# One more row pair of the spatial product by one level of Strassen, with the buffers and the order around it

## The chip, the cores and the metric

The kernel runs on one core of a Trainium2 chip. The metric is the device time of one launch in microseconds (us), as the median of several runs. The engines are named as in the profile: PE is the matrix engine, PEld its weight loads, DVE the vector engine, ACT the scalar engine, POOL the GpSimd engine, and SP the engine that only issues transfers here.

## The reference

Two branches work on the same `x` (2048 tokens x 512) and are mixed by a sigmoid gate per token. Branch A is a linear attention with 32 heads of 16 columns; branch B a gated MLP whose gate mixes tokens with the 2048 x 2048 matrix `w_sp`.

```python
# A: for each head, phi_q and phi_k are softmax(+p) and softmax(-p) of q @ w_phi, k @ w_phi
kv  = einsum('bhsf,bhsd->bhfd', phi_k, v)
z   = einsum('bhsf->bhf', phi_k)
o   = einsum('bhqf,bhfd->bhqd', phi_q, kv) / (einsum('bhqf,bhf->bhq', phi_q, z)[..., None] + 1e-6)
a   = o.reshape(B, S, D) @ wo
# B: z = gelu(x @ w_in), z1 and z2 are its halves of 688 columns
g2  = einsum('ts,bsf->btf', w_sp, layernorm(z2)) + b_sp[None, :, None]
b   = (z1 * g2) @ w_out
g   = sigmoid((x * gate_w).sum(-1))
out = g * a + (1 - g) * b
```

## The kernel before

Tokens are worked on in 16 tiles of 128. There are three stages, and in each the order of PE and of ACT is written out by hand in the Python code, while the order on DVE, POOL and SP is made by a scheduler from priorities.

**First stage** (`z2_tile`, `z1_tile`, `fold`): both halves of `x @ w_in`, gelu, the layernorm of z2 into `z2all` (fp16), the sums of z2's blocks `T1` to `T4` into `zmix`, and `w_phi` folded into the weights of k and q.

**The spatial product** `w_sp @ z2` goes by pairs of row tiles p and p + 8, p = 0 to 7. `w_load` brings both row tiles of a pair, transposed, into one of three buffers `wsp`. A pair in `PLAIN` takes four steps of `plain` (L523), one for each row tile and half of the columns (344), each of 16 matmuls, and DVE adds the bias and multiplies by z1 in place (L531). A pair in `MIXED` takes seven `product`s (L553) of 8 matmuls each, by the Winograd form of one Strassen level. The pair's block matrix is A11, A12 (row tile p) and A21, A22 (row tile p + 8), each 128 rows by 1024 tokens; z2 is cut the same way into B11 to B22. Ahead of its products such a pair needs:

- `w_size` twice (L342): ACT sums absolute values of a half of the pair, one pass over 128 x 2048 each; `w_level` (L351): one small matmul adds over partitions, and DVE makes the factors `wdown` and `wup` (L352, L355); `w_scale` (L370): ACT scales A21 and A22 in place to fp16.
- `w_sum`: S3 = A11 - A21 and S4 = A12 - S2 (L358, DVE), S1 = A21 + A22 (L375, POOL), S2 = A22 - S3 (L377, DVE). S2 and S3 lie in `wmix`.

Three PSUM banks `mm0` to `mm2` hold the products. Products 6, 7 and 4 add onto one bank, and ACT reads it after each of them (`scaled`), so the next one may not start before that read. Product 1 of a following pair is taken between 6 and 7, and `seed` copies it into the second bank. `plus` (DVE) and `gated` (POOL, L573) finish each quarter into z1, which is then called u.

**kv stage**: a loop over 16 tiles. Each turn makes k of the next tile (`k_tile`), v of this one, adds to the 128-wide kv sums (`kv_acc`, two tiles late), and does one entry of `steps`; every second or third turn it makes a tile of q. The steps of pairs 0 to 4 fall here. Step 16 on fall into the output stage.

**Output stage**: first three turns of product, `attn_tile`, `q_tile`; then for each of 16 tiles in pair order (`token`) `ba_tile` (o @ wo and u @ w_out into one bank), one product and one q tile or what is left (`FILL`), `attn_tile` four tiles ahead, and `u_T`. `attn_tile` multiplies q by kv into the bank pair `kvat`, of which there is one only: DVE must have read it (L609, L610) before the next `attn_tile` may write it; before the first one DVE must have taken the kv sums out of it (`kvz_evac`, L500, L505). SP transposes q (`eqT`, L471), o (`oT`, L619) and u (`uT`, L520) by DMA.

In the kernel before, pairs 0 and 5 are in `PLAIN`. Pair 0's four steps are at turns 0 to 3 of the kv stage, pair 5's at the passage from the kv stage to the output stage (three of them each stand ahead of one of the first three `attn_tile`s).

Of the kernel before, what the change touches and what calls it, by code (L numbers as in the profile page):

```python
# [14 lines left out]
P = 128  # L15
# [16 lines left out]
WP = 704  # L32
NP = NT // 2
HS = NT // 2
NRING = 3
PLAIN = (0, 5)
MIXED = (1, 2, 3, 4, 6, 7)
LEVEL = 2.0 ** -15


# [1 line left out]
def kernel(  # L42
# [130 lines left out]
    for p in range(NRING):  # L173
        w_load(p)
    nc.gpsimd.memset(mhalf[:], -0.5)
    nc.gpsimd.memset(mask4[:], 1.0)
# [160 lines left out]
        return [lambda: take(dst[:, 3], banks[3]), lambda: take(dst[:, 2], banks[2])]  # L337

    def w_size(p, h):
        if h == 0:  # L340
            wmix[p] = ring.tile([P, 2, HS, P], FP16, name="wmix", bufs=2)
        nc.scalar.activation(  # L342
            out=wmix[p].bitcast(BF16).rearrange("p k s c -> p (k s c)"),
            in_=wraw[p][:, h * NT:(h + 1) * NT, :].rearrange("p s c -> p (s c)"),
            func=AF.Abs, accum_out=wsum[:, p, h:h + 1])
        if h == 1:
            nc.vector.tensor_tensor(
                out=wsum16[:, p:p + 1], in0=wsum[:, p, 0:1], in1=wsum[:, p, 1:2], op=ALU.add)

    def w_level(p, ps):  # L350
        nc.tensor.matmul(ps[:, 0:1], lhsT=ones_sq[:, :], rhs=wsum16[:, p:p + 1], start=True, stop=True)  # L351
        nc.vector.tensor_scalar(  # L352
            out=wdown[:, p:p + 1], in0=ps[:, 0:1], scalar1=LEVEL, scalar2=1e-30,
            op0=ALU.mult, op1=ALU.max)
        nc.vector.reciprocal(out=wup[:, p:p + 1], in_=wdown[:, p:p + 1])  # L355

    def w_mul_sub(out, raw, p, minus):
        nc.vector.scalar_tensor_tensor(  # L358
            out=out, in0=raw, scalar=wup[:, p:p + 1], in1=minus, op0=ALU.mult, op1=ALU.subtract)

    def w_part(p, name):
        if name in ("S2", "S3"):
# [7 lines left out]
        nc.scalar.activation(out=tail.bitcast(FP16), in_=tail, func=AF.Copy, scale=wup[:, p:p + 1])  # L370

    def w_sum(p, k):
        a21, a22, s2, s3 = (w_part(p, name) for name in ("A21", "A22", "S2", "S3"))
        if k == 1:
            S1_ENG.tensor_tensor(out=a21, in0=a21, in1=a22, op=ALU.add)  # L375
        elif k == 2:
            nc.vector.tensor_tensor(out=s2, in0=a22, in1=s3, op=ALU.subtract)  # L377
        elif k == 3:
            w_mul_sub(s3, w_part(p, "A11"), p, a21)
        else:  # L380
            w_mul_sub(w_part(p, "S4"), w_part(p, "A12"), p, s2)
# [9 lines left out]
    def z_sum(part, i):  # L391
# [5 lines left out]
    S1_ENG = nc.gpsimd  # L397
# [28 lines left out]
    def bank_tile(tag):  # L426
        return psM.tile([P, CH], FP32, name="mm", tag=tag)
# [88 lines left out]
            nc.sync.dma_start(out=w_out_sb[0:REM, 5, :], in_=B_w_out[5 * P:FH, :])  # L516

    def u_T(n):
        uT = work.tile([P, NFT, P], BF16, name="uT", bufs=NUT)
        nc.sync.dma_start_transpose(out=uT[:, :, :], in_=z1all[:, token(n), :])  # L520
        uTs[n] = uT

# [8 lines left out]
        nc.vector.scalar_tensor_tensor(  # L531
            out=zu, in0=x, scalar=bT[:, t:t + 1], in1=zu, op0=ALU.add, op1=ALU.mult)

    LEAD = {6: 1, 7: 1}
    LOAD_AT = {3: 4, 4: 7, 5: 10, 6: 13, 7: 16}
    PRODUCTS = {1: (0, "A11", "B11"), 6: (1, "S2", "T2"), 5: (2, "S1", "T1"), 2: (0, "A12", "B21"),
                7: (1, "S3", "T3"), 4: (1, "A22", "T4"), 3: (2, "S4", "B22")}
    OPENS, SEEDED = (1, 5), (6, 7, 4)
# [58 lines left out]
    def attn_tile(n):  # L597
        at = psM.tile([P, 8, P], FP32, name="at", tag="kvat", bufs=1)
        for g in range(8):
            nc.tensor.matmul(  # L600
                at[:, g, 0:AW], lhsT=eqTs[n][:, g, :], rhs=kvz[:, g, :], start=True, stop=True)
        rden = work.tile([P, 8, NG], FP32, name="rden", tag="rden")
        o = work.tile([P, D], BF16, name="o")
        o_out(n, o[:].rearrange("p (u h d) -> p u h d", u=8, d=DH), at[:, :, 0:AW], rden, NG)
        o_T(n, o)

    def o_out(n, o, at, rden, nh):
# [61 lines left out]
    def at(n, *todo):  # L669
        work_at.setdefault(n, []).append(todo)  # L670

    for p in range(NP):
        n, after = len(steps), MIXED[MIXED.index(p) + 1:][:1] if p in MIXED else ()
        if p in PLAIN:
            steps += [[(plain, t, j)] for t in (p, p + HS) for j in range(2)]
            continue
        opened = p - 1 in MIXED
        follow = [(product, q, 1) for q in after if q == p + 1]
        first = [(product, p, 1)] * (not opened) + [(product, p, 5), (product, p, 2)]
        middle = [(product, p, 6)] + follow + [(product, p, 7)]  # L680
# [9 lines left out]
    for p in range(NRING, NP):  # L690
        at(LOAD_AT[p], w_load, p)

    for i, n in enumerate((1, 2)):
# [7 lines left out]
    def level(n):  # L701
        for f, p, *_ in work_at.get(n, ()):
            if f is w_scale:
                w_level(p, bank_tile(Q_BANK if n < NT else X_TAGS[2]))

    FILL = [("p", "q")] * 6 + [("p", "qp"), ("p", "p")] + [("p", "")] * 4 + [("", "")] * 3
    Q_AT = (1, 3, 6, 9, 12, 15)
    with tc.manual_schedule(engines={mybir.EngineType.PE, mybir.EngineType.Activation}):
        ks = {0: k_tile(0, Q_BANK)}
        kvacc = psM.tile([P, 8, P], FP32, name="kvacc", tag="kvat", bufs=1)  # L710
        pend = []
        for tt in range(NT):
# [7 lines left out]
            pend.append((tt, ek, v_tile(tt, rk, V_BANK if tt != 1 else X_TAGS[2])))  # L720
            level(tt)
            prepare(tt, w_sum)
            if len(pend) == 3:
                kv_acc(*pend.pop(0))
            for i, part in enumerate(steps.pop(0)):
                part[0](*part[1:])
                if i == 0:
                    prepare(tt, w_scale, *[w_size] * late)
            if tt in Q_AT:
                q_tile(Q_AT.index(tt), bank_tile(Q_BANK))  # L730
        nc.scalar.activation(out=g_el[:, :], in_=glog[:, :], func=AF.Exp)
        nc.vector.tensor_scalar(out=g_1p[:, :], in0=g_el[:, :], scalar1=1.0, scalar2=None, op0=ALU.add)
        nc.vector.reciprocal(out=g_inv[:, :], in_=g_1p[:, :])
# [7 lines left out]
    with tc.manual_schedule(engines={mybir.EngineType.PE, mybir.EngineType.Activation}):  # L741
        wo_t = st2.tile([P, NG, D], BF16, name="wo_t", bufs=1)
        nc.gpsimd.dma_start(out=wo_t[:, :, :], in_=A_wo.rearrange("(g p) n -> p g n", p=P))
        todo, done_steps = [], [0]
        x_tags = list(X_TAGS)

        def products(n):
            for _ in range(n):
                if not todo and steps:
                    todo.extend(steps.pop(0))  # L750
                    n = NT + done_steps[0]
                    done_steps[0] += 1
                    level(n)
                    prepare(n, w_sum)
                    f, *args = todo.pop(0)
                    f(*args)
                    prepare(n, w_load, w_size, w_scale)
                elif todo:
                    f, *args = todo.pop(0)
                    f(*args)  # L760
# [62 lines left out]
```

## Time and profile before

| what | value |
|---|---|
| median of three runs | 201.99 us (201.79 to 203.42) |
| the profiled execution's own time | 202.68 us |
| its span | 200.3 us |
| PE busy | 194.9 us, 97% of the span |
| DVE busy | 139.5 us, 70% |
| ACT busy | 126.7 us, 63% |
| POOL busy | 93.0 us, 46% |
| granted PE clock | 1.0 in all of the span |
| L527, matmuls of the plain pairs | 128 |
| L559, matmuls of the mixed pairs | 144 + 96 + 96 |

The span is what the instructions cover; the execution's own time has 2.4 us more around it. A group's "mean ns of one" on PE includes the tail of a pipelined matmul; how long a row of matmuls holds PE is read from the starts in the timeline.

### The profile page before, as it was taken

How to read it: one execution, taken by the hardware profiler on the slowest of the kernel's cores; microseconds unless marked ns; L12 is line 12 of the kernel's file. 1: busy time of each engine (PE TensorE's matmuls, PEld its weight loads, DVE VectorE, ACT ScalarE, POOL GpSimd, SP SyncE). 2: the span in 40 equal slices, each digit the busy share in tenths (PEclk: the TensorE clock that was granted, in tenths of full speed). 3: DMA queues.
4: the chain of work that ended last, by engine and by line, in shares of the span. 5: the costliest groups of instructions: out<-in, count | busy, mean ns of one | idle time of the engine just before them, and what ended most of it. 6: DMA issues, size and time to landing. Idle time of an engine off the chain costs nothing.

```text
span 200.3 us, 3991 instructions
## 1 busy us (share of the span) xinstructions
PE 194.9 (97%) x1473; PEld 116.8 (58%) x1491; DVE 139.5 (70%) x260; ACT 126.7 (63%) x199; POOL 93.0 (46%) x134
## 2 busy tenths in 40 slices
PE   7999999999999999999999999999999999999994
PEld 3666666665555665565565656655555555556542
DVE  4379877914988977887887974999698666633500
ACT  3466667889849759959957469576844455224222
POOL 6021123000665765986985979266058244421300
PEclk9999999999999999999999999999999999999999
DMA  6899489998053930980990844983948988793261
GB/s 183 142 199 217 75 196 198 159 196 236 1 43 77 224 57 0 186 157 0 197 145 3 168 94 119 184 170 69 155 101 170 164 177 168 149 147 78 80 151 58
DMA packets 89210, 26.50 MB, mean 132 GB/s; under 512 B 84536, under 2 KB 89064, under 8 KB 89192
## 3 DMA queue, kind: packets, MB, share of 16 engines
q1 hardware_dynamic: 86448, 23.32, 61.8%
q10 hardware_dynamic: 2600, 2.42, 4.2%
q0 software_dynamic: 144, 0.52, 1.0%
q8 instruction: 11, 0.18, 0.4%
q14 instruction: 7, 0.06, 0.1%
HBM read 3.45 MB, written 2.10 MB: 28 GB/s over the span
## 4 chain that ended last, share of the span: by engine, by line
PE 89%; DVE 4%; ACT 3%; DMA 2%; issue 1%; SPq 0%; DVEq 0%
PE mm L559 24%; PE zp L208 19%; PE mm L434 12%; PE mm L629 10%; PE mm L624 7%; PE mm L477 6%; PE mm L527 6%; PE at L600 2%; DMA w_z<-in_B_w_in_dram 2%; PE kvacc L494 2%; ACT wmix L342 2%; DVE zs L442 1%; DVE o L610 1%; DVE wmix L358 1%; ACT eq L438 0%
## 5 line engine op out<-in xcount | busy, mean ns | idle before, releaser
L208 PE MATMUL zp<-w_z,xT 128*128 128x344 bf16 (+1 forms) x254 | 38.3, 311 | 0.3 <-DMA w_z<-in_B_w_in_dram 0.3
L208 PEld LDWEIGHTS <-xT 128*128 128x128 bf16 x254 | 24.5, 98 | 12.0
L559 PEld LDWEIGHTS <-wsp 128*128 128x128 f16 (+1 forms) x240 | 22.9, 98 | 12.2 <-issue 0.5
L573 POOL TENSOR_TENSOR z1all<-c,z1all 128x344 bf16<-128x344 f32 x24 | 22.8, 960 | 15.2 <-DVE c L566 11.7
L641 ACT ACTIVATE ob<-mm,g_inv 128x512 bf16<-128x512 f32 (+1 forms) x16 | 10.9, 681 | 22.6 <-PE mm L629 20.0
L559 PE MATMUL mm<-z2all,wsp 128*128 128x344 f16 x144 | 23.9, 309 | 0.0
L442 DVE TENSOR_REDUCE zs<-ek 128x64 f32<-128x1024 bf16 x16 | 19.0, 1193 | 7.0 <-ACT ek L438 7.0
L438 ACT ACTIVATE eq<-mm 128x512 bf16<-128x512 f32 x32 | 17.3, 594 | 10.3 <-PE mm L434 6.5
L442 DVE TENSOR_REDUCE zs<-eq 128x64 f32<-128x1024 bf16 x16 | 19.4, 1214 | 5.7 <-ACT eq L438 5.5
L629 PE MATMUL mm<-w_out_sb,uT 128*128 128x512 bf16 (+2 forms) x101 | 23.3, 366 | 0.1
L342 ACT ACTIVATE wmix<-wsp 128x2048 bf16<-128x2048 bf16 x12 | 23.0, 1918 | 0.0
L527 PE MATMUL mm<-z2all,wsp 128*128 128x344 f16 x128 | 20.0, 309 | 0.0
L375 POOL TENSOR_TENSOR wsp<-wsp 128x1024 f16<-128x1024 f16 x6 | 12.8, 2126 | 13.8 <-DVE wmix L358 13.8
L457 POOL TENSOR_TENSOR ratio<-zs,rk 128x32 f32<-128x32 f32 x16 | 7.5, 466 | 23.7 <-DVE rk L451 21.1
L434 PEld LDWEIGHTS <-xT 128*128 128x128 bf16 x128 | 11.8, 98 | 10.5
L438 ACT ACTIVATE ek<-mm 128x512 bf16<-128x512 f32 x32 | 17.3, 601 | 1.1 <-PE mm L434 1.1
L458 POOL TENSOR_TENSOR eq<-eq,ratio 128x512 bf16<-128x512 bf16 x16 | 16.9, 1058 | 1.3
L458 POOL TENSOR_TENSOR ek<-ek,ratio 128x512 bf16<-128x512 bf16 x16 | 16.9, 1059 | 0.0
L223 ACT ACTIVATE z2raw<-zp 128x688 bf16<-128x688 f32 x16 | 11.8, 744 | 7.6 <-PE zp L208 7.3
L629 PEld LDWEIGHTS <-uT 128*128 128x128 bf16 x102 | 9.8, 98 | 11.2 <-DMA uT<-z1all 0.2
L624 PE MATMUL mm<-wo_t,oT 128*128 128x512 bf16 (+2 forms) x66 | 16.3, 366 | 0.1
L434 PE MATMUL mm<-wk_p,xT 128*128 128x512 bf16 x61 | 16.1, 379 | 0.2
(100 smaller groups left out, 322.8 us busy)
## 6 DMA issues: line engine op xcount, KB each, us to landing
out_dram<-ob ACTq DMA_DIRECT2D x14, 128.0 KB, 2.6
w_z<-in_B_w_in_dram SPq DMA_DIRECT2D x2, 344.0 KB, 5.1
w_out_sb<-in_B_w_out_dram SPq DMA_DIRECT2D x1, 640.0 KB, 5.4
wv_sb<-in_A_wqkv_dram SPq DMA_DIRECT2D x1, 512.0 KB
wo_t<-in_A_wo_dram POOLq DMA_DIRECT2D x1, 512.0 KB, 4.5
w_z<-in_B_w_in_dram ACTq DMA_DIRECT2D x2, 172.0 KB, 3.9
w_z<-in_B_w_in_dram SPq DMA_DIRECT2D x2, 172.0 KB, 4.0
wsp<-in_B_w_sp_dram SPq DMA_TRANSPOSE x16, 5.2
```

Of the source, the lines that this page charges most:

```text
L208: nc.tensor.matmul(zp[:, j, 0:n], lhsT=xT[:, dt, tt * P:(tt + 1) * P], rhs=wt[:, dt, j * HF:j * HF + n], start=(dt == 0), stop=(dt == NDT ...
L342: nc.scalar.activation(out=wmix[p].bitcast(BF16).rearrange("p k s c -> p (k s c)"), in_=wraw[p][:, h * NT:(h + 1) * NT, :].rearrange("p s ...
L375: S1_ENG.tensor_tensor(out=a21, in0=a21, in1=a22, op=ALU.add)
L434: nc.tensor.matmul(ps[:, :], lhsT=xT[:, dt, tt * P:(tt + 1) * P], rhs=w[:, dt, :], start=(dt == 0), stop=(dt == NDT - 1))
L438: nc.scalar.activation(out=e[:, :, a, :], in_=ps[:, :].rearrange("p (h f) -> p h f", f=DH), func=AF.Exp, scale=1.0 - 2.0 * a)
L442: nc.vector.tensor_reduce(out=z[:].rearrange("p h a -> p (h a)"), in_=e[:].rearrange("p h a f -> p (h a) f"), axis=AX.X, op=ALU.add,)
L458: nc.gpsimd.tensor_tensor(out=e[:, :, 1, :], in0=e[:, :, 1, :], in1=ratio[:, :, None].to_broadcast([P, H, DH]), op=ALU.mult)
L527: nc.tensor.matmul(x, lhsT=wraw[t % HS][:, h * NT + st, :], rhs=z2all[:, st, j * HF:(j + 1) * HF], start=(st == 0), stop=(st == NT - 1))
L559: nc.tensor.matmul(x, lhsT=w_part(p, wa)[:, st, :], rhs=zsums[zb][:, st, :], start=(k in OPENS and st == 0), stop=(st == HS - 1), skip_gro ...
L573: nc.gpsimd.tensor_tensor(out=zu, in0=o, in1=zu, op=ALU.mult)
L624: nc.tensor.matmul(acc, lhsT=oTs[n][:, g, :], rhs=wo_t[:, g, c0:c1], start=start and g == 0, stop=stop and g == NG - 1)
L629: nc.tensor.matmul(acc, lhsT=uTs[n][:, ft, :], rhs=w_out_sb[:, ft, c0:c1], start=start and ft == 0, stop=stop and ft == NFT - 1)
```

## The change

Pair 5 moves from `PLAIN` to `MIXED`. All of pairs 1 to 7 now chain: each pair's product 1 stands between products 6 and 7 of the pair before, so pair 5's product 1 is in the kv stage, and the output stage has 20 products (pairs 5, 6 and 7) in place of four plain steps and 14 products. In the passage one product stands ahead of the first `attn_tile` and two ahead of the second and third.

- There are four `wsp` buffers in place of three, and pairs 3 to 7 are loaded three turns earlier. `w_size` writes its unused result into a buffer of its own (`mute`), not into `wmix`, and `wmix` is taken when S3 is formed. The turns of `w_size` and `w_scale` are moved.
- `uT` and `oT` move to the pool `st2`, which takes the room that the kv stage's pools leave. The transfers that fill them can then not start in the kv stage.
- S3 and S4 are formed in two halves each. S1 of pair 6 is formed by DVE, the others still by POOL.
- `wdown` and `wup`, `kvz_evac` and the two DVE operations of `attn_tile` get high priority for the scheduler. The gate's factors are formed at turn 2 of the kv stage.
- `FILL` and the places of the level matmul are adapted.

```diff
-NRING = 3
-PLAIN = (0, 5)
-MIXED = (1, 2, 3, 4, 6, 7)
+NRING = 4
+PLAIN = (0,)
+MIXED = (1, 2, 3, 4, 5, 6, 7)
...
-        if h == 0:
-            wmix[p] = ring.tile([P, 2, HS, P], FP16, name="wmix", bufs=2)
+        mute = ring.tile([P, NT * P], BF16, name="mute", bufs=1)
         nc.scalar.activation(
-            out=wmix[p].bitcast(BF16).rearrange("p k s c -> p (k s c)"),
+            out=mute[:, :],
...
     def w_mul_sub(out, raw, p, minus):
-        nc.vector.scalar_tensor_tensor(
-            out=out, in0=raw, scalar=wup[:, p:p + 1], in1=minus, op0=ALU.mult, op1=ALU.subtract)
+        for c in (slice(0, HS // 2), slice(HS // 2, HS)):
+            nc.vector.scalar_tensor_tensor(
+                out=out[:, c, :], in0=raw[:, c, :], scalar=wup[:, p:p + 1], in1=minus[:, c, :],
+                op0=ALU.mult, op1=ALU.subtract)
...
     def w_sum(p, k):
+        if k == 3:
+            wmix[p] = ring.tile([P, 2, HS, P], FP16, name="wmix", bufs=2)
...
         if k == 1:
-            S1_ENG.tensor_tensor(out=a21, in0=a21, in1=a22, op=ALU.add)
+            (nc.vector if p == 6 else nc.gpsimd).tensor_tensor(out=a21, in0=a21, in1=a22, op=ALU.add)
...
-        uT = work.tile([P, NFT, P], BF16, name="uT", bufs=NUT)
+        uT = st2.tile([P, NFT, P], BF16, name="uT", bufs=NUT)
...
-    LEAD = {6: 1, 7: 1}
-    LOAD_AT = {3: 4, 4: 7, 5: 10, 6: 13, 7: 16}
+    LOAD_AT = {3: 1, 4: 4, 5: 7, 6: 10, 7: 13}
+    SIZE_AT = {1: (0, 1, 2), 2: (2, 3, 4), 6: (14, 16, 17), 7: (18, 19, 20)}
...
-        o_out(n, o[:].rearrange("p (u h d) -> p u h d", u=8, d=DH), at[:, :, 0:AW], rden, NG)
+        with tc.high_priority():
+            o_out(n, o[:].rearrange("p (u h d) -> p u h d", u=8, d=DH), at[:, :, 0:AW], rden, NG)
...
-        oT = work.tile([P, NG, P], BF16, name="oT", bufs=7)
+        oT = st2.tile([P, NG, P], BF16, name="oT", bufs=7)
...
-        n -= LEAD.get(p, 0)
-        at(n - 4, w_size, p, 0)
-        at(n - 3, w_size, p, 1)
-        at(n - 2, w_scale, p)
+        s0, s1, s2 = SIZE_AT.get(p, (n - 5, n - 4, n - 3))
+        at(s0, w_size, p, 0)
+        at(s1, w_size, p, 1)
+        at(s2, w_scale, p)
...
-                w_level(p, bank_tile(Q_BANK if n < NT else X_TAGS[2]))
+                w_level(p, bank_tile(K_BANK if NT <= n < NT + 4 else Q_BANK))
 
-    FILL = [("p", "q")] * 6 + [("p", "qp"), ("p", "p")] + [("p", "")] * 4 + [("", "")] * 3
+    FILL = [("p", "q")] * 7 + [("p", ""), ("p", "p"), ("p", ""), ("p", ""), ("p", "p")] + [("", "")] * 3
...
-        kvz_evac()
+        with tc.high_priority():
+            kvz_evac()
...
         for n in range(3):
-            products(1)
+            products(1 + (n > 0))
             attn_tile(n)
             q_next()
```

More of the change, by code (lines that the diff above doesn't have):

```diff
@@ L171, in w_load @@
                 out=wraw[p][:, h * NT:(h + 1) * NT, :], in_=B_w_sp[t * P:(t + 1) * P, :])
-    for p in range(NRING):
+    for p in range(3):
         w_load(p)
@@ L351, in w_level @@
         nc.tensor.matmul(ps[:, 0:1], lhsT=ones_sq[:, :], rhs=wsum16[:, p:p + 1], start=True, stop=True)
[L352 to L355, printed above, removed]
+        with tc.high_priority():
+            nc.vector.tensor_scalar(
+                out=wdown[:, p:p + 1], in0=ps[:, 0:1], scalar1=LEVEL, scalar2=1e-30,
+                op0=ALU.mult, op1=ALU.max)
+            nc.vector.reciprocal(out=wup[:, p:p + 1], in_=wdown[:, p:p + 1])
     def w_mul_sub(out, raw, p, minus):
-        nc.vector.scalar_tensor_tensor(
-            out=out, in0=raw, scalar=wup[:, p:p + 1], in1=minus, op0=ALU.mult, op1=ALU.subtract)
+        for c in (slice(0, HS // 2), slice(HS // 2, HS)):
+            nc.vector.scalar_tensor_tensor(
+                out=out[:, c, :], in0=raw[:, c, :], scalar=wup[:, p:p + 1], in1=minus[:, c, :],
+                op0=ALU.mult, op1=ALU.subtract)
     def w_part(p, name):
@@ L395, in z_sum @@
             out=zsums[out][:, c, :], in0=zsums[a][:, c, :], in1=zsums[b][:, c, :], op=op)
-    S1_ENG = nc.gpsimd
     with tc.manual_schedule(engines={mybir.EngineType.PE, mybir.EngineType.Activation}):
@@ L685 @@
             at(n + lag, w_sum, p, k)
-        n -= LEAD.get(p, 0)
-        at(n - 4, w_size, p, 0)
-        at(n - 3, w_size, p, 1)
-        at(n - 2, w_scale, p)
-    for p in range(NRING, NP):
+        s0, s1, s2 = SIZE_AT.get(p, (n - 5, n - 4, n - 3))
+        at(s0, w_size, p, 0)
+        at(s1, w_size, p, 1)
+        at(s2, w_scale, p)
+    for p in range(3, NP):
         at(LOAD_AT[p], w_load, p)
@@ L720 @@
             pend.append((tt, ek, v_tile(tt, rk, V_BANK if tt != 1 else X_TAGS[2])))
+            if tt == 2:
+                nc.scalar.activation(out=g_el[:, :], in_=glog[:, :], func=AF.Exp)
+                nc.vector.tensor_scalar(
+                    out=g_1p[:, :], in0=g_el[:, :], scalar1=1.0, scalar2=None, op0=ALU.add)
+                nc.vector.reciprocal(out=g_inv[:, :], in_=g_1p[:, :])
             level(tt)
@@ L724 @@
                 kv_acc(*pend.pop(0))
-            for i, part in enumerate(steps.pop(0)):
+            parts = steps.pop(0)
+            for i, part in enumerate(parts):
                 part[0](*part[1:])
                 if i == 0:
-                    prepare(tt, w_scale, *[w_size] * late)
+                    prepare(tt, *[w_size] * late)
+                if i == 0:
+                    prepare(tt, w_scale)
             if tt in Q_AT:
                 q_tile(Q_AT.index(tt), bank_tile(Q_BANK))
-        nc.scalar.activation(out=g_el[:, :], in_=glog[:, :], func=AF.Exp)
-        nc.vector.tensor_scalar(out=g_1p[:, :], in0=g_el[:, :], scalar1=1.0, scalar2=None, op0=ALU.add)
-        nc.vector.reciprocal(out=g_inv[:, :], in_=g_1p[:, :])
         for p_ in pend:
             kv_acc(*p_)
-        kvz_evac()
+        with tc.high_priority():
+            kvz_evac()
     kvp_cm.__exit__(None, None, None)
@@ L748, in products @@
             for _ in range(n):
-                if not todo and steps:
+                opening = not todo
+                if not todo:
+                    if not steps:
+                        return
                     todo.extend(steps.pop(0))
-                    n = NT + done_steps[0]
                     done_steps[0] += 1
[L753 to L760, printed above, removed]
+                now = NT + done_steps[0] - 1
+                if opening:
+                    level(now)
+                    prepare(now, w_sum)
+                f, *args = todo.pop(0)
+                f(*args)
+                if opening:
+                    prepare(now, w_size)
+                if not todo:
+                    prepare(now, w_scale)
         def q_next():
```

## The prediction

> **What bounds the kernel now.** I read the busy table first, then the waits of PE, then the windows of the passage from the kv stage to the output stage (busy us of each engine in stretches of 4 us), then the timeline there.
>
> ```profile
> PE 194.9 (97%) x1473; PEld 116.8 (58%) x1491; DVE 139.5 (70%) x260; ACT 126.7 (63%) x199; POOL 93.0 (46%) x134
> ```
>
> ```profile
> PE zp L239 <- PEq L807: 0.8, 1, 0.8
> PE at L600 <- DVE o L610: 0.4, 1, 0.4
> PE zp L208 <- DMA w_z<-in_B_w_in_dram: 0.3, 1, 0.3
> ```
>
> ```profile
> 124.00:128.00 4.00, 3.95 (x34) 2.56 (x33) 3.75 (x10) 1.75 (x6) 2.16 (x4) 1.00 0.96 120
> 128.00:132.00 4.00, 4.00 (x34) 2.57 (x33) 3.84 (x8) 3.56 (x5) 1.47 (x3) 1.00 1.24 255
> 132.00:136.00 4.00, 3.57 (x30) 2.15 (x29) 4.00 (x8) 2.98 (x6) 2.77 (x2) 1.00 0.58 115
> 136.00:140.00 4.00, 4.00 (x32) 2.31 (x30) 3.90 (x10) 2.27 (x4) 2.49 (x4) 1.00 0.37 71
> ```
>
> In the windows the columns are PE, PEld, DVE, ACT and POOL. PE is the bound. Between the first loads and the end it waits once, in the passage, and there DVE is busy for 15.5 of 16 us. So time can be had only by fewer matmuls or by that one wait, and DVE in the passage has no room. The wait in the timeline:
>
> ```profile
> 130.68 2.50 PE L527 MATMUL mm<-z2all,wsp 128*128 128x344 f16 x16
> 130.77 1.97 DVE L358 SCALAR_TENSOR_TENSOR wmix<-wsp,wup 128x1024 f16<-128x1024 bf16 x1
> ...
> 132.67 0.74 DVE L610 SCALAR_TENSOR_TENSOR o<-at,g_el,rden 128x512 bf16<-128x512 f32 x1
> ...
> 133.56 0.42 PE L600 MATMUL at<-kvz,eqT 128*128 128x68 bf16 x8 [0.38 <-DVE o L610]
> ...
> 137.00 0.42 PE L600 MATMUL at<-kvz,eqT 128*128 128x68 bf16 x8
> ```
>
> The third `attn_tile` (at2, counting from 0) could have started at 130.68 + 2.33 = 133.01; it started at 133.56, 0.15 us after DVE's o ended at 133.41. **0.55 us** were lost. The reader should see why: S3 (L358) took 1.97 us where the other five took 1.28, and o stood behind it. The fourth (at3) started at 137.00. From at3 on both kernels have the same PE work: 14 products, the same attention, q and output tiles. PE has no wait there before. So **the change is worth what at3 moves**, plus any new wait later.
>
> **PE's work.** Row starts give what a group holds PE: 8 matmuls of 344 columns 1.17 us (112.28 to 113.44), 16 of them 2.33, k, v or q 0.86, `kv_acc` or `attn_tile` 0.26, the level matmul 0.03. Pair 5 goes from 64 matmuls to 56: 8 x 0.146 = **-1.17**, with one more level **+0.03**. If the old wait of 0.55 went as well and none came, the change would be worth -1.69.
>
> **Until the kv stage ends.** Before, turn 13 has products 5, 2 and 6 and k of tile 15 starts at 115.78. After, product 6 stands in turn 14, so that k starts at 114.61, and PE goes on with v (115.47), kv (116.33), pair 4's product 6 (116.59), pair 5's product 1 (117.76), pair 4's product 7 (118.92), v of tile 15 (120.09), kv (120.95). Product 4 could start at 121.2. It waits for ACT to have read product 7, and ACT has between the reads of 6 and 7 a `w_size` (1.90, and 0.20 for its sum): 117.76 + 0.2 to start + 0.64 + 2.1 + 0.64 = 121.35. Turns 8 and 11 have that order too, but there a k tile of 0.86 covers it; turn 15 has no k. **+0.2**. Then products 4 and 3, q, two kv sums: 125.1. Product 5 of pair 5 covers `kvz_evac`: 0.2 to start, 0.68 and 0.18, done at 126.2; at0 at 126.3 (before 126.08).
>
> The rest of pair 5's preparation in the kv stage I cost at nothing. ACT gets two `w_size` and a `w_scale` (6.2 us) in turns 11 to 13; the pattern is that of turns 5 to 10, where the trace of before has the same operations over three turns and no wait of PE. S1 on POOL (2.13) has from about 119.7 to 125.1. The level matmul stands right behind a q tile in turns 4, 7, 10 and 13 and needs that q's bank; before, ACT was done with q at 96.70 in the turn like it and v ended at 96.84, so this cover is thin: 0 to +0.1 each time. I take 0. Each `w_load` goes into the buffer of the pair that ended one turn before it, three turns ahead of where it was, and SP has then no uT in its queue. The gate's factors (0.22 on ACT, 0.4 on DVE) and a `w_size` of pair 2 fall into turn 2, where ACT stood idle 2.98 us until its `w_scale` at 59.32; the buffer `mute` is written by ACT alone. If that idle time were not there, 2.3 us of ACT would stand ahead of turn 3's k, which is used a turn (5 us) later.
>
> **From at0 to at3, DVE's queue.** In the order of the changed program DVE has, from the end of `kvz_evac` to the o that frees the bank for at3: three sums of q (L442, a start-to-start of 1.2 each) 3.6; three reciprocals of them, 0.28 each, 0.85; three rden at 0.33, 1.0; three o at 0.68, 2.1; wdown and wup 0.35; one `plus` 0.45; S4 of pair 5 in two halves 1.25. Sum **9.6**: 126.2 + 9.6 = 135.8, and with the 0.15 from above at3 starts at 135.95. PE alone would be there at 126.3 + 9.23 = 135.5 (three at, three q, five products, a level). The plain tiles' multiply (0.5 each) is gone from DVE, but 1.17 us of PE's work, its cover, went too. at3 moves from 137.00 to 135.95: **-1.05**, if nothing on DVE is stretched.
>
> S4 may be. Its row:
>
> ```profile
> L358 DVE SCALAR_TENSOR_TENSOR wsp<-wsp,wup,wmix x6: 1179/1236/2150, 69.5 to 174.5; 128x1024 f16<-128x1024 bf16 x6
> ```
>
> The 2150 ns one started at 69.48, at the same time as a POOL multiply (69.49, 1.06 us). Three of the eighteen operations of S2, S3 and S4 are stretched so (1.97, 2.15, 1.75). Unstretched is one end, +0.97 (2.15 - 1.18) the other. By the walk POOL's multiply of q runs from about 128.4 to 129.4, and the first half of S4 would start at 128.7; so I take the middle, **+0.5**. S3, S2 and S1 of pair 6 follow at3 and have cover: S1 on DVE (no row shows it; bounds 0.62 of S2 and 2.13 of POOL's S1) ends some 5.6 us after at3 starts, and the product that needs it comes 6.85 after.
>
> The Trainium skill, "SBUF — State Buffer", section "Who interferes with whom", speaks against this change: a DVE instruction with two SBUF inputs and a GpSimd instruction that reads SBUF exclude each other, and the later waits for the whole of the earlier. The rows above agree in kind. By that rule each half of S4 could be held by a multiply of its own, 2.1 us in all, and at3 would come at 138.0, +1.0; by the rows of stretched whole operations it comes at 136.9, -0.1.
>
> **uT and oT.** The first `uT` waits for the kv sum of tile 13 (121.4) and v's multiply. SP then issues five uT (1.24 each, with gaps 1.3), 121.4 to 128; then q's transpose, ready from POOL at 129.4, then the first oT at 130.8, which lands in 2.6 us (median of L619): 133.4. The first `ba_tile` wants it at 136.2. Slack 2.8. At the end `uT` of tile 14 is wanted 5.16 us after the last product, before it was 5.42 (now the last `attn_tile` stands ahead of that product); the trace needs 1.79 to its issue (188.37 to 190.16) and 3.1 to land, so 0.3 is left: 0.
>
> **Sum.** -1.05 + 0.5 = **-0.55** against the profiled execution: 202.68 becomes 202.1, its span 200.3 becomes 199.75. That execution lies 0.7 over the median; on the median 201.99 - 0.55 gives **201.4**. The forecast's own range is 200.9 to 202.0.
>
> **Rivals.**
> - *PE is fed all through.* DVE's order may fit better than my walk, and the waits go. For it: S4 and S3 were unstretched in ten of twelve. Against it: DVE's 9.6 against PE's 9.23. at3 at 135.5: -1.5, **200.5**.
> - *DVE and POOL block each other in the passage.* One mechanism: six more POOL multiplies (0.84 each) and two more DVE operations with both inputs in SBUF, in a queue that is full. S4 stretched costs 0.97 ahead of at3; after it S3's two halves and S1 stretched by up to 1.0 each end S1 at 5.6 + 3.0 = 8.6 after at3, and product 5 of pair 6, wanted at 6.85, is 1.75 late: -1.05 + 0.97 + 1.75 = +1.7. With two of the three stretched +0.7. Middle **203.0**. It decides from the point where S1 of pair 6 ends over 6.85 us after at3. Against it: only three of eighteen such rows.
> - *SP's queue is late.* Four of the uT behind a busy ring take 2.1 us as one did at 156.31, and the first oT stands behind them and behind q's transpose. 5 x 2.2 from 121.4 ends at 132.4, oT issues at 133.8 and lands at 136.4 to 137.2 (3.4 is the longest): up to 1.0 on the forecast, **202.3**. Against it: the last `wsp` load, which filled the rings at 122.6 to 128.9 before, now is over by then.
>
> That the products aren't fewer can be left out: the built program has 392 + 64 such matmuls in place of 336 + 128.
>
> **Chances.** Forecast 0.50, PE fed 0.15, DVE against POOL 0.18, SP 0.09, something that I don't see 0.08. The range **200.3 to 203.0** leaves out the outer half of the third case, most of the last, and a little below. About 1%, 2.0 us, is what a measurement of this kernel can tell from no change. Faster by that needs under 199.97, more than the whole -1.69: 0.03. Slower needs over 204.0, the far end of the third case or the unseen: 0.12. Within: 0.85.
>
> **What the profile would show.** Right: no wait of PE over 0.3 us in the kv stage; at3 near 136.4; PE's only wait in the passage an `attn_tile` on DVE's o; L561 with 392 matmuls. Wrong: a wait of a product on DVE's S1 or S3, of a `ba_tile` on oT or uT, or of the level matmul on ACT.

## The result, and the profile after

The changed kernel takes 203.09 us (median of 22 runs, 202.62 to 204.39) against 201.96 us of the kernel before: a ratio of **1.005** with a 95% interval of 1.0033 to 1.0068. The forecast was 201.4. The kernel got half a per cent slower, although the eight matmuls that were to be saved are saved.

In this document GpSimd is the profile's POOL and VectorE its DVE. First the busy table and the waits of PE after the change (us in total, times, longest).

```profile
PE 193.5 (96%) x1466; PEld 115.6 (57%) x1484; DVE 152.3 (75%) x279; ACT 134.6 (67%) x209; POOL 96.4 (48%) x138
```

```profile
PE mm L561 <- DVE c L568: 1.2, 2, 0.7
PE mm L350 <- DVE wsum L346: 0.9, 1, 0.9
PE zp L239 <- PEq L820: 0.8, 1, 0.8
PE pq L310 <- DMA gaterow<-in_gate_w_dram: 0.7, 1, 0.7
PE zp L208 <- DMA w_z<-in_B_w_in_dram: 0.6, 1, 0.6
```

PE is busy 1.4 us less. The wait of an `attn_tile` on DVE's o, the only one that PE had behind the first loads before, is gone. Two new lines stand on top: products that wait for `plus` (L568), and a level matmul that waits for a size (L346). The other three lie in the first stage. To see where they lie I cut PE's timeline at three places: the start of the first k tile, the first `attn_tile` (at0) and the fourth (at3).

| kernel | median us | ratio to before (95%) | first k to at0 | at0 to at3 | at3 to the end of the last matmul |
|---|---|---|---|---|---|
| before | 201.96 | 1 | 81.86 | 10.92 | 60.45 |
| after | 203.09 | 1.005 (1.0033 to 1.0068) | 84.04 | 9.33 | 60.44 |
| after, second profile (a2) | 203.26 | 1.0048 (1.0011 to 1.0084) | 84.07 | 9.33 | 60.70 |
| e1: size added by a reduce | 201.72 | 0.9973 (0.9949 to 0.9996) | 82.67 | 9.34 | 60.71 |
| e2: size of pair 2 a turn later | 203.91 | 1.0083 (1.0059 to 1.0106) | 84.93 | 9.34 | 60.43 |
| **e3: every S1 on DVE** | **199.72** | **0.9867 (0.9828 to 0.9906)** | 81.56 | 9.34 | 60.44 |
| e4: S3, S4 whole | 201.08 | 0.9959 (0.9922 to 0.9996) | 81.62 | 9.21 | 60.85 |
| b1: before, every S1 on DVE | 201.38 | 0.9962 (0.9947 to 0.9977) | 81.32 | 10.91 | 60.45 |
| b2: before, S3 and S4 in halves | 205.70 | 1.0171 (1.0145 to 1.0198) | 84.00 | 12.19 | 60.43 |
| e8: e3 and an idle add on POOL | 206.08 | 1.0198 (1.0178 to 1.0218) | 87.19 | 9.33 | 60.44 |
| e9: e3 and an idle copy on POOL | 201.02 | 0.9946 (0.9924 to 0.9968) | 82.61 | 9.33 | 60.44 |
| e13: S1 of 1, 2, 5, 6 on DVE | 200.45 | 0.9916 (0.9889 to 0.9944) | 81.54 | 9.33 | 60.45 |
| e10: e3 with pair 5 plain | 204.26 | 1.0124 (1.0077 to 1.0171) | 81.87 | 16.48 | 58.97 |
| e11: e3 and e4 | 200.49 | 0.992 (0.9893 to 0.9947) | 81.62 | 9.21 | 61.18 |

A run named e changes the kernel after, a run named b the kernel before. Each ratio is to runs of the kernel before that were taken beside it on the same chip (their medians: 201.96 for after, 202.09 for e1 to e4, 202.23 for b1, b2, e8 and e9, 202.12 for the other four). The three stretches are read from one profiled execution of each kernel.

So the passage gained 1.59 us, and the kv stage, where PE's work is the same but for one level matmul (0.03) and the preparation of the pairs was rearranged, lost 2.18. Against e3, in which PE has the same order of work, the loss is visible tile by tile (v tiles counted from the first k): 1.18 us in turn 4, 0.45 in turn 6, 0.86 in turn 15, nothing elsewhere. These are 2.49 in all; e3 itself is 0.30 below the kernel before in this stage.

The timeline of the kernel after around turn 4, all engines (start, us, engine, line, operation; in brackets the idle time before):

```profile
64.78 2.12 POOL L379 TENSOR_TENSOR wsp<-wsp 128x1024 f16<-128x1024 f16 x1 [3.07 <-issue]
...
65.04 1.88 DVE L346 TENSOR_TENSOR wsum<-wsum 128x1 bf16<-128x1 f32 x1
65.11 1.03 PE L479 MATMUL mm<-wv_sb,xT 128*128 128x512 bf16 x4
...
67.07 0.16 PE L350 MATMUL mm<-wsum,ones_sq 128*128 128x1 bf16 x1 [0.93 <-DVE wsum L346]
```

The reader should look at the second line. It adds two columns of 128 numbers, one element for each partition, and takes 1.88 us; the shortest of its seven executions takes 98 ns. It starts inside POOL's S1 and ends at 66.92, POOL's S1 at 66.90. In the kernel before, S1 of this pair ran from 62.72 to 64.84 and the size of pair 2 was added at 69.40, in 0.16 us:

```profile
62.72 2.12 POOL L375 TENSOR_TENSOR wsp<-wsp 128x1024 f16<-128x1024 f16 x1 [2.01 <-DVE wmix L358]
...
69.40 0.16 DVE L347 TENSOR_TENSOR wsum<-wsum 128x1 bf16<-128x1 f32 x1 [0.36 <-ACT wmix L342]
```

The same in turn 15 of the kernel after, with S2 (L381) in the place of the size, and `plus` (L568) behind it:

```profile
122.00 2.12 POOL L379 TENSOR_TENSOR wsp<-wsp 128x1024 f16<-128x1024 f16 x1 [0.63 <-DVE wmix L359]
122.31 2.37 DVE L381 TENSOR_TENSOR wmix<-wsp,wmix 128x1024 f16<-128x1024 f16 x1
...
123.19 1.33 PE L561 MATMUL mm<-zmix,wsp 128*128 128x344 f16 x8
...
124.60 0.56 DVE L568 SCALAR_TENSOR_TENSOR c<-mm,wdown,u 128x344 f32<-128x344 f32 x1
125.22 1.04 PE L561 MATMUL mm<-z2all,wsp 128*128 128x344 f16 x6 [0.69 <-DVE c L568]
```

S2 takes 2.37 us, and again it ends (124.68) soon after POOL's S1 (124.12): the 0.56 us between them are a little less than the 0.62 of the shortest free S2. Product 3 could have started 1.17 after product 4, at 124.36, and started at 125.22. The trace's answer for S2 alone, min/median/max in ns, then the first and last start:

```profile
L381 DVE TENSOR_TENSOR wmix<-wsp,wmix x7: 676/1770/2367, 67.3 to 169.3; 128x1024 f16<-128x1024 f16 x7
```

Six of the seven take over 1.5 us; before, the median was 682 ns. The first, at 67.33 (1.51 us), runs beside POOL's multiply of k and not beside S1; the other five run beside S1.

### The profile page after: what moved, and what is told of

Same layout as the page of the kernel before. It is cut to its first block, busy times and chain, and to the rows that moved or that the text cites. A ratio compares the mean times of both kernels' runs of the same rounds, so it can differ in the third digit from the quotient of the medians.

```text
span 201.8 us, 4016 instructions
## 1 busy us (share of the span) xinstructions
PE 193.5 (96%) x1466; PEld 115.6 (57%) x1484; DVE 152.3 (75%) x279; ACT 134.6 (67%) x209; POOL 96.4 (48%) x138
## 4 chain that ended last, share of the span: by engine, by line
PE 79%; DVE 9%; issue 4%; ACT 4%; DMA 2%; DVEq 0%
PE mm L561 23%; PE zp L208 18%; PE mm L436 10%; PE mm L632 10%; PE mm L627 7%; PE mm L479 4%; PE mm L529 2%; DVE zs L444 2%; DMA gaterow<-in_gate_w_dram 2%; PE at L602 2%; DVE vr L485 1%; PE kvacc L496 1%; DVE wmix L359 1%; DVE wmix L381 1%; ACT ek L440 1%
## 5 line engine op out<-in xcount | busy, mean ns | idle before, releaser
L561 PEld LDWEIGHTS <-wsp 128*128 128x128 f16 (+1 forms) x280 | 26.7, 98 | 15.5 <-issue 1.6
L575 POOL TENSOR_TENSOR z1all<-c,z1all 128x344 bf16<-128x344 f32 x28 | 25.2, 905 | 13.6 <-DVE c L568 7.2
L561 PE MATMUL mm<-z2all,wsp 128*128 128x344 f16 x168 | 27.9, 309 | 1.2 <-DVE c L568 1.2
L341 ACT ACTIVATE mute<-wsp 128x2048 bf16<-128x2048 bf16 x14 | 26.8, 1914 | 0.4 <-ACT ob L644 0.4
L459 POOL TENSOR_TENSOR ratio<-zs,rk 128x32 f32<-128x32 f32 x16 | 7.0, 437 | 25.6 <-DVE rk L453 20.3
L561 PE MATMUL mm<-zmix,wsp 128*128 128x344 f16 x112 | 18.6, 309 | 0.0
L561 PE MATMUL mm<-zmix,wmix 128*128 128x344 f16 x112 | 18.6, 309 | 0.0
L372 ACT ACTIVATE wsp<-wsp,wup 128x2048 f16<-128x2048 bf16 x7 | 14.0, 2000 | 5.6 <-DVE wup L355 5.6
L460 POOL TENSOR_TENSOR ek<-ek,ratio 128x512 bf16<-128x512 bf16 x16 | 17.4, 1085 | 0.0
L479 PE MATMUL mm<-wv_sb,xT 128*128 128x512 bf16 x62 | 16.3, 379 | 0.1
```

The source lines that it names most:

```text
L341: nc.scalar.activation(out=mute[:, :], in_=wraw[p][:, h * NT:(h + 1) * NT, :].rearrange("p s c -> p (s c)"), func=AF.Abs, accum_out=wsum[: ...
L460: nc.gpsimd.tensor_tensor(out=e[:, :, 1, :], in0=e[:, :, 1, :], in1=ratio[:, :, None].to_broadcast([P, H, DH]), op=ALU.mult)
L479: nc.tensor.matmul(v_ps[:, :], lhsT=xT[:, dt, tt * P:(tt + 1) * P], rhs=wv_sb[:, dt, :], start=(dt == 0), stop=(dt == NDT - 1))
L561: nc.tensor.matmul(x, lhsT=w_part(p, wa)[:, st, :], rhs=zsums[zb][:, st, :], start=(k in OPENS and st == 0), stop=(st == HS - 1), skip_gro ...
L575: nc.gpsimd.tensor_tensor(out=zu, in0=o, in1=zu, op=ALU.mult)
```

## The theory and its rivals

**T:** while POOL reads SBUF, a DVE operation with two inputs in SBUF does not run. The change moved S1 (POOL) so that it now runs at the same time as the size of pair 2 (turn 4) and as S2 ahead of `plus` (turns 6 and 15), and PE waits soon after for what stands behind them. **R1:** the size is asked for a turn too early, and POOL has nothing to do with it. **R2:** it is the order and the splitting on DVE alone. **R3:** the first stage got longer too (first k at 44.88 us after, 44.22 before). **R4:** S1 on DVE is simply faster, whatever the change. **R5:** S1's cost is by what waits for its result or by its place in POOL's queue, and no operation of DVE gets longer by it.

## Experiments

### e1: the size added with one input

```diff
-            nc.vector.tensor_tensor(
-                out=wsum16[:, p:p + 1], in0=wsum[:, p, 0:1], in1=wsum[:, p, 1:2], op=ALU.add)
+            with nc.allow_low_precision("sum of two"):
+                nc.vector.tensor_reduce(
+                    out=wsum16[:, p:p + 1], in_=wsum[:, p, 0:2], op=ALU.add, axis=mybir.AxisListType.X)
```

> One edit to the changed kernel: the two halves of a w_sp row's size are added by a tensor_reduce over the pair of columns (one input in SBUF) instead of a tensor_tensor (two inputs in SBUF); the order on every engine stays. Theory T (in the kv stage GpSimd's S1 now runs beside VectorE operations with two SBUF inputs that PE soon waits for): the size of pair 2 takes 0.1 to 0.3 us instead of 1.88 although S1 of pair 1 still runs, the level matmul of turn 4 follows the v tile without its wait, everything after it is 1.0 to 1.1 us earlier: ratio to the kernel before 1.000 (0.998 to 1.002). The waits of products 3 in turns 6 and 15 stay. Rival R1 (the size is asked for a turn too early, GpSimd has nothing to do with it): the wait of the level matmul stays near 0.9 us, ratio 1.005.

It took 201.72 us, 1.4 less than the changed kernel; at0 came 1.37 us earlier. The timeline of e1 at the same place:

```profile
63.90 2.13 POOL L380 TENSOR_TENSOR wsp<-wsp 128x1024 f16<-128x1024 f16 x1 [3.07 <-issue]
64.16 0.09 DVE L347 TENSOR_REDUCE wsum<-wsum 128x1 bf16<-128x2 f32 x1
...
64.65 1.92 DVE L382 TENSOR_TENSOR wmix<-wsp,wmix 128x1024 f16<-128x1024 f16 x1
...
65.08 0.17 PE L351 MATMUL mm<-wsum,ones_sq 128*128 128x1 bf16 x1
```

The same sum, at the same point in DVE's order, in the middle of the same S1, takes 0.09 us when its two numbers come in as one operand, and the level matmul waits for nothing. R1 falls. The next operation with two operands, S2, is held in its place (1.92), where PE does not wait for it. The waits for `plus` stay (1.0 us), as expected.

### e2: the size of pair 2 a turn later

```diff
-    SIZE_AT = {1: (0, 1, 2), 2: (2, 3, 4), 6: (14, 16, 17), 7: (18, 19, 20)}
+    SIZE_AT = {1: (0, 1, 2), 2: (3, 4, 5), 6: (14, 16, 17), 7: (18, 19, 20)}
```

> One edit to the changed kernel: SIZE_AT of pair 2 is (3, 4, 5) as in the kernel before, so its level matmul stands in turn 5. T and R1 both expect the wait of turn 4 to go: ratio to the kernel before 0.999 to 1.001 (1.0 to 1.1 us less than the changed kernel), provided the size is not met by S1 of pair 1 again (S1 is at 64.8 to 66.9 us from the span's start, the size a turn later, near 70). If the wait only moves to turn 5 or to the scaling that stands behind it, ratio 1.003 to 1.005. The waits of products 3 in turns 6 and 15 stay.

A miss: 203.91 us, slower than the changed kernel. The scheduler laid out DVE anew, and the meeting moved to the next pair, in turn 7:

```profile
81.10 2.12 POOL L379 TENSOR_TENSOR wsp<-wsp 128x1024 f16<-128x1024 f16 x1 [1.22 <-ACT mute L341]
81.35 1.89 DVE L346 TENSOR_TENSOR wsum<-wsum 128x1 bf16<-128x1 f32 x1
...
83.39 0.16 PE L350 MATMUL mm<-wsum,ones_sq 128*128 128x1 bf16 x1 [0.34 <-DVE wsum L346]
```

Two products also wait for ACT (0.9 us together): in turn 5 a size of pair 3 and the scaling of pair 2 now stand one behind the other, 73.51 to 77.39, ahead of the read that product 4 needs. With a scheduler between the code and the engine, moving one operation is not one edit.

### e3: every S1 on DVE

```diff
-            (nc.vector if p == 6 else nc.gpsimd).tensor_tensor(out=a21, in0=a21, in1=a22, op=ALU.add)
+            nc.vector.tensor_tensor(out=a21, in0=a21, in1=a22, op=ALU.add)
```

> One edit to the changed kernel: S1 of every pair on VectorE (1.12 us there for the one that is already there) instead of GpSimd (2.12 us for each of five in the kv stage); VectorE gets some 6 us more work in the kv stage and the order of the rest stays nearly as it is. T: the size of pair 2 takes 0.1 to 0.2 us, S2 0.7 us, the halves of S3 and S4 near 0.7; the wait of the level matmul in turn 4 goes (-1.1 us) and those of products 3 in turns 6 and 15 shrink by the difference of 2.37 and 0.7 + 1.1 (-0.4 to -0.6 each): ratio to the kernel before 0.995 to 0.998. Rival R2 (it is the order on VectorE, S2 ahead of the sum with the decoded bank and S3 in two halves with other work between them; more work there makes it worse): waits stay or grow, ratio 1.005 to 1.015.

199.72 us, ratio 0.9867, below what T expected, and **2.4 us faster than the kernel before**. The list of PE's waits has one line left, in the first stage:

```profile
PE zp L239 <- PEq L820: 0.8, 1, 0.8
```

Turn 15, in e3's timeline:

```profile
119.83 0.62 DVE L379 TENSOR_TENSOR wsp<-wsp 128x1024 f16<-128x1024 f16 x1
120.38 0.75 DVE L381 TENSOR_TENSOR wmix<-wsp,wmix 128x1024 f16<-128x1024 f16 x1
...
121.05 0.56 DVE L568 SCALAR_TENSOR_TENSOR c<-mm,wdown,u 128x344 f32<-128x344 f32 x1
121.87 1.33 PE L561 MATMUL mm<-z2all,wsp 128*128 128x344 f16 x8
```

S1 and S2 together take less on DVE (1.22 us to the start of `plus`) than S2 alone did beside POOL's S1 (2.29). DVE's busy time falls from 152.3 to 148.2 us, although it does six more operations. R2, which expected more work on DVE to make it worse, falls in that form.

### e4: S3 and S4 in one instruction again

```diff
-        for c in (slice(0, HS // 2), slice(HS // 2, HS)):
+        for c in (slice(0, HS),):
```

> One edit to the changed kernel: S3 and S4 are one instruction each again instead of two halves (VectorE's order is planned anew; S1 of pair 1 can then start some 2 us earlier, as in the kernel before, 62.7 instead of 64.8 us). T: what counts is whether S1 runs beside the size of pair 2, so the wait of turn 4 goes or shrinks to 0.2 us (-0.9 to -1.1 us), those of turns 6 and 15 stay, the passage is up to 0.3 us worse: ratio 0.999 to 1.003. R1: wait in turn 4 stays, ratio 1.005 to 1.007.

201.08 us, below what either theory expected: all the waits of the kv stage are gone, those of turns 6 and 15 too, which I had expected to stay. With whole operations the scheduler makes another order; in turn 6 it puts S3 of pair 2 ahead of S4 of pair 1, and S1 starts 2.8 us ahead of S2 in place of 1.0. Timeline of e4 there:

```profile
71.96 1.85 DVE L359 SCALAR_TENSOR_TENSOR wsp<-wsp,wup,wmix 128x1024 f16<-128x1024 bf16 x1
72.69 3.10 POOL L379 TENSOR_TENSOR wsp<-wsp 128x1024 f16<-128x1024 f16 x1
75.46 0.89 DVE L381 TENSOR_TENSOR wmix<-wsp,wmix 128x1024 f16<-128x1024 f16 x1
```

Here the one that comes later is POOL: S1 starts at 72.69, but S4 runs until 73.81, and so S1 takes 3.10 us. It ends at 75.79 and holds S2 for 0.2 us only. In turn 15 S2 starts first (119.09, 0.78 us), and S1 (119.28) is the one held: it takes 2.57. So the split is what brought S1 and S2 together, through the order that came of it, and the hold is the price: R2 is right about the cause of the meeting.

### b1 and b2: one part alone in the kernel before

```diff
-    S1_ENG = nc.gpsimd
+    S1_ENG = nc.vector
```

> The kernel before with one edit: S1 of every pair on VectorE, as in the run e3 of the changed kernel. Theory T (S1 on GpSimd holds VectorE operations that PE waits for, in the changed kernel alone; in the kernel before S2 stands behind the sum with the decoded bank and the size behind S1's end, so PE never waits): no gain to be had here, 201.5 to 202.4 us, ratio 0.998 to 1.002. Rival R4 (S1 on VectorE is worth some 2.4 us by itself, and the seventh pair brings nothing even with the waits gone): ratio 0.985 to 0.992.

201.38 us, ratio 0.9962: more than T's none, far less than R4's 2.4 us. At0 comes 0.54 us earlier, in three steps of 0.18 (turns 6, 9 and 12): the old kernel lost a little to S1 on POOL too, in gaps too small for the list of waits. Between b1 and e3 stands the change without S1's holds: 201.38 to 199.72, with intervals of the ratios that do not touch. In the trace 0.24 us are lost in the kv stage (0.19 of them in turn 6) and 1.57 won in the passage.

```diff
-        nc.vector.scalar_tensor_tensor(
-            out=out, in0=raw, scalar=wup[:, p:p + 1], in1=minus, op0=ALU.mult, op1=ALU.subtract)
+        for c in (slice(0, HS // 2), slice(HS // 2, HS)):
+            nc.vector.scalar_tensor_tensor(
+                out=out[:, c, :], in0=raw[:, c, :], scalar=wup[:, p:p + 1], in1=minus[:, c, :],
+                op0=ALU.mult, op1=ALU.subtract)
```

> The kernel before with one part of the change alone: S3 and S4 in two halves each. S2 still stands behind the sum with the decoded bank on VectorE, and S1 of pair 1 does not move (both halves of that S3 stand together). T: S1 comes up to 0.7 us later in the other pairs, S2 is held for it up to 0.7 us, nothing of it reaches PE: ratio 0.999 to 1.003. Rival R2 (the split by itself is what costs the 2 us that undoing it gave back in e4): ratio 1.006 to 1.012.

205.70 us, ratio 1.0171: both theories were far too low. The list of PE's waits in b2:

```profile
PE at L602 <- DVE o L612: 1.6, 1, 1.6
PE mm L561 <- ACT u L543: 1.5, 2, 0.8
```

S2 is held by S1 here as well (79.08, 1.68 us), but that is not the path. Half of an S4 stands ahead of a k tile's reciprocal now and takes 1.40 us beside a multiply on POOL; the factor wup comes 0.63 us later (89.67 against 89.04), ACT starts the pair's scaling later by as much, and ACT's read of product 7 stands behind the scaling: product 4 waits 0.74. In the passage half of an S3 (1.44) makes o late. So the split in itself costs 3.5 us in the old order; in the changed kernel the factor has high priority, and this path does not show.

### e8 and e9: an operation that nobody waits for

```diff
-            (nc.vector if p == 6 else nc.gpsimd).tensor_tensor(out=a21, in0=a21, in1=a22, op=ALU.add)
+            nc.vector.tensor_tensor(out=a21, in0=a21, in1=a22, op=ALU.add)
+            if p != 6:
+                extra = ring.tile([P, HS, P], FP16, name="extra", bufs=1)
+                nc.gpsimd.tensor_tensor(out=extra[:, :, :], in0=a22, in1=s3, op=ALU.add)
```

> The run e3 (S1 on VectorE, 199.72 us) with one thing added: GpSimd adds A22 and S3 of pairs 1, 2, 3, 4, 5, 7 into a tile that nobody reads, in the place on GpSimd where S1 stood, with the same shapes; VectorE's order is that of e3 to the last instruction. T: VectorE operations with two SBUF inputs are held by it as by S1: size of pair 2 near 1.8 us, S1 and S2 on VectorE together held once, and the waits of the level matmul in turn 4 and of products 3 in turns 6 and 15 come back, the latter longer by S1's own 0.7 us: ratio to the kernel before 1.002 to 1.010 (+3 to +4.7 us over e3). Rival R5 (S1 cost by what waits for its result, or by the place in GpSimd's queue ahead of the products with z1, not by holding VectorE): ratio 0.985 to 0.991, no operation of VectorE longer than in e3.

206.08 us, 6.4 above e3 and more than T's upper end. Turn 4 and turn 9 of e8:

```profile
64.10 2.12 POOL L382 TENSOR_TENSOR extra<-wsp,wmix 128x1024 f16<-128x1024 f16 x1 [3.06 <-issue]
64.35 1.88 DVE L346 TENSOR_TENSOR wsum<-wsum 128x1 bf16<-128x1 f32 x1
...
92.46 2.12 POOL L382 TENSOR_TENSOR extra<-wsp,wmix 128x1024 f16<-128x1024 f16 x1 [0.62 <-DVE wmix L359]
92.77 2.36 DVE L379 TENSOR_TENSOR wsp<-wsp 128x1024 f16<-128x1024 f16 x1
...
96.34 0.89 PE L564 MATMUL mm<-z2all,wsp 128*128 128x344 f16 x5 [0.50 <-DVE c L571]
```

No result of `extra` is used, and the size takes 1.88 us, to the digit as in the changed kernel; S1 (L379) is held in S2's stead in five more places. PE waits for the size (0.9) and four times for `plus` (3.4 together), now in turns 9 and 12 too. R5 falls: DVE's operations are what got longer, and PE waits for them. It is the hold.

```diff
-                nc.gpsimd.tensor_tensor(out=extra[:, :, :], in0=a22, in1=s3, op=ALU.add)
+                nc.gpsimd.tensor_copy(out=extra[:, :, :], in_=s3)
```

> As the run e8, but GpSimd's extra instruction is a copy of S3 into the tile that nobody reads (one input in SBUF) in place of the addition. T as the page on SBUF states it (any GpSimd instruction that reads SBUF holds a VectorE instruction with two SBUF inputs): held as in e8, in proportion to the copy's length, ratio above that of e3 by 0.5 to 2%. If only GpSimd instructions with two inputs do it: 0.986 to 0.990 as e3, with the size at 0.1 us and S2 near 0.7 us beside the copy.

201.02 us, 1.3 above e3. A POOL instruction with one input holds as well, for as long as it runs itself:

```profile
63.91 1.04 POOL L382 COPY extra<-wmix 128x1024 f16<-128x1024 f16 x1 [3.00 <-DVE wmix L359]
64.23 0.73 DVE L346 TENSOR_TENSOR wsum<-wsum 128x1 bf16<-128x1 f32 x1
```

The size ends at 64.96, the copy at 64.95. That is what the Trainium skill, "SBUF — State Buffer", section "Who interferes with whom", states of a GpSimd instruction that reads SBUF, and it agrees with e1's reduce too: by that section a VectorE instruction with one SBUF input does not contend with GpSimd, outside the modes that use two ports, and a `tensor_reduce` has none of these on this chip.

### a2, e13, e10, e11

a2 is the changed kernel unaltered.

> The changed kernel as it is, for a second profile. Its first k tile began at 44.88 us in the first profile and at 43.99 to 44.34 in every other kernel, in a stage whose code is the same. If that is a matter of one execution, the first k tile begins at 44.0 to 44.4 here, the stretch from there to the first attention tile is 84.0 again and the passage 9.3. Rival R3 (the change makes the first stage longer): 44.7 or later again. Ratio 1.003 to 1.007.

The first k began at 44.01 us this time; 84.07 and 9.33 came again. R3 falls.

```diff
-            (nc.vector if p == 6 else nc.gpsimd).tensor_tensor(out=a21, in0=a21, in1=a22, op=ALU.add)
+            (nc.gpsimd if p in (3, 4, 7) else nc.vector).tensor_tensor(out=a21, in0=a21, in1=a22, op=ALU.add)
```

> The changed kernel with S1 on VectorE for pairs 1, 2, 5 and 6 (as it was for 6) and on GpSimd for 3, 4 and 7. T in numbers: e3 gained 1.18 us in turn 4 (pair 1), 0.45 in turn 6 (pair 2) and 0.86 in turn 15 (pair 5) over the changed kernel and nothing in turns 9 and 12 (pairs 3 and 4), although S2 takes 2.37 us there; so 2.49 us are gained here as in e3: first attention tile 81.5 to 81.7 us after the first k tile, ratio 0.986 to 0.991. If what the holds cost adds up over all pairs: a third of the gain is missing, ratio 0.991 to 0.996.

At0 comes 81.54 us after the first k: all of e3's gain in the kv stage, with three pairs still on POOL. The ratio, 0.9916, lies just inside the range of the other expectation, and its interval takes in both; I go by the trace, since the time between its first k and its end is that of e3 to 0.1 us. In turn 9 of e13:

```profile
89.68 2.13 POOL L379 TENSOR_TENSOR wsp<-wsp 128x1024 f16<-128x1024 f16 x1 [0.63 <-DVE wmix L359]
89.98 2.37 DVE L381 TENSOR_TENSOR wmix<-wsp,wmix 128x1024 f16<-128x1024 f16 x1
...
92.28 0.56 DVE L568 SCALAR_TENSOR_TENSOR c<-mm,wdown,u 128x344 f32<-128x344 f32 x1
92.89 1.33 PE L561 MATMUL mm<-z2all,wsp 128*128 128x344 f16 x8
```

S2 is held for its full 2.37 us, and product 3 still follows product 4 (91.72) after 1.17. A hold costs only where its cover is gone.

```diff
-PLAIN = (0,)
-MIXED = (1, 2, 3, 4, 5, 6, 7)
+PLAIN = (0, 5)
+MIXED = (1, 2, 3, 4, 6, 7)
```

> The run e3 with the seventh pair undone: rows 5 and 13 of w_sp by plain products again (64 matmuls of 344 columns instead of 56), the rest of the change as it is, S1 on VectorE. T: the pair is worth its 8 matmuls once nothing waits, 8 x 0.146 = 1.17 us, and the 0.4 us wait that the passage before had: 1.2 to 1.6 us slower than e3, ratio to the kernel before 0.992 to 0.996. Rival (the gain of e3 is S1's place and the order alone): within 0.3 us of e3, ratio 0.985 to 0.989.

Inconclusive: 204.26 us, 4.5 above e3. The turns of the sizes and the fill of the output stage fit a mixed pair 5; a level matmul in the passage waits 1.9 us for its size. The granted clock was also only 0.93 from 120 to 140 us in its profiled execution. Between b1 and e3 (1.66 us) lies all of the change but the holds; what of it is the pair's alone and what the buffers, priorities and order around it bring, no run separates.

e11 has the edits of e3 and e4 together.

> The edits of e3 and e4 together: S1 of all pairs on VectorE, S3 and S4 in one instruction each. T: in e3 PE waits for nothing more between the first k tile and the end, so there is nothing left for the second edit: within 0.4 us of e3, ratio 0.985 to 0.990. If the halves cost by themselves (R2), up to 1 us below e3: ratio 0.982 to 0.985.

200.49 us, ratio 0.992. The kv stage is as in e3; the passage is 0.13 shorter, the output stage 0.7 longer in its one profile. No gain over e3; its ratio is a little above the 0.990 of my limit, and what made the output stage longer stays open.

## Why the prediction was wrong, point by point

- **PE is the bound, and the change is worth what at3 moves, plus any new wait later.** Right as far as it goes: from at3 on the kernels take 60.45 us before and 60.44 after (60.70 in the second profile of after). I then looked for new waits in the wrong stretch.
- **The step that failed: "The rest of pair 5's preparation in the kv stage I cost at nothing."** The kv stage took 2.18 us more than before, where the sum had +0.2. I priced S1 as "S1 on POOL (2.13) has from about 119.7 to 125.1", that is by who waits for its result. It ran there, 122.00 to 124.12, and its result was in time; what it cost is that S2 could not run beside it (0.86 in turn 15, against e3). The other two losses against e3, 1.18 in turn 4 and 0.45 in turn 6, are not pair 5's at all: the halves of S3 and S4 (with them alone undone, in e4, these waits are gone) and the earlier turn of pair 2's size moved operations of pairs 1 and 2, and I gave the rearrangement of pairs that were mixed already no term of its own.
- **The mechanism was in the prediction, in the wrong place.** I had the row of the S4 that took 2150 ns, the rule cited beside it, and a rival "DVE and POOL block each other in the passage". In the passage it did little harm: the first half of S4 was stretched there (1.52 us; the second half took 0.73), and S1 of pair 6 ended 6.02 us after at3, before the 6.85 from which the rival was to decide. The rival's own middle was added wrongly: +0.7 and +1.7 on 201.99 have it at 203.2, not 203.0.
- **The passage.** at0 to at3 was to take 9.65 + 0.5 = 10.15 us, 0.77 less than before; it took 9.33, 1.59 less. Mis-sized was DVE's 9.6 us from the end of `kvz_evac` to the o ahead of at3. It took 9.45 with a stretch of 0.8 in it (128.66 to 138.11), so 8.65 without: I had added durations of seventeen operations, and in the trace these overlap their neighbours by 0.07 to 0.09 us in all places but one. at3 did start right behind that o (138.25), so the limit was named rightly, but DVE was just in time: at0 to at3 took 9.33, against 9.23 of PE's work alone. The rival "PE is fed all through", with -1.5, was right for this stretch.
- **The 0.2 us at product 4 in turn 15** did not occur: product 4 follows the kv sum without a gap (122.94, 123.19).
- **uT, oT and the last tiles:** right. SP issued five uT from 123.39 to 130.33 and the first oT at 133.17, and no `ba_tile` waited; the SP rival found nothing.
- **What the profile was to show.** The sign of being right failed: waits of 0.93, 0.48 and 0.69 us in the kv stage, and at3 at 138.25 (137.41 in the second profile), not near 136.4. None of the three signs of being wrong came either: the products waited for `plus`, which stood behind S2, and the level matmul for DVE's size, not for ACT.
- **Sum.** Kv stage +2.18 and passage -1.59 give +0.59 where I had +0.2 and -0.75. The medians differ by 1.13. Of the rest 0.25 lies behind the last matmul (3.11 us to the end of the span against 2.85, also in the second profile); some 0.3 I can't place; the 0.25 by which the second profile is longer from at3 to the last matmul may be part of it.

The range, 200.3 to 203.0, missed by 0.1, and the sign was wrong. That it missed by so little is no merit: its upper end came from a rival that did not occur.

## What to carry to other kernels

Before you move or split an operation on VectorE or GpSimd, list for both engines which operations have two inputs in SBUF (VectorE) or read SBUF at all (GpSimd), and lay the two orders side by side: here what an operation held cost more than what waited for its result, and a short one that PE needed soon was the worst to be held. Try the same operation on VectorE as well: six additions of 2.12 us on GpSimd became 0.62 to 0.68 us each on VectorE and made VectorE less busy. Price a rearrangement of the old work by itself, apart from the new work that it makes room for.

## What the runs showed that I had not expected

- An addition of one element per partition took 1.88 us on VectorE, against 0.09 to 0.1 alone, because GpSimd was adding 128 x 1024 elements; as a reduce over the two columns it took 0.09 beside the same instruction.
- The held size ends within 0.02 us of the instruction that holds it in all four cases (after, e2, e8, e9); a longer one then takes its own time (S2: 0.56 more). It works the other way too: S1 on GpSimd took 3.10 us behind an S4.
- Splitting S3 and S4 in halves, with nothing else changed, cost the kernel before 3.5 us, the largest effect of the parts that were tried alone, and it works through the order that the scheduler then makes.
